# Two partial sums out of one PSUM bank: twelve value products and every sixth gate of a fused Fourier-mixing and gated feed-forward kernel

## The chip, the cores and the metric

The kernel runs on one core of one Trainium2 chip. The metric is device time of one launch in microseconds (µs), smaller is better. Engines are named as the profile names them: PE is the matrix engine and PEld its weight loads, DVE the vector engine, ACT the scalar engine, POOL is GpSimd, SP only issues DMAs. PSUM is the memory that PE writes its products into; the kernel splits it into eight banks of 128 × 512 float32.

## The reference

```
X   = real(fft(fft(x, axis=1), axis=2))      # x: 8 batches x 3008 rows x 256 channels
x2  = X.reshape(24064, 256)
out = (relu(x2 @ w_gate) * (x2 @ w_val)) @ w_out   # w_gate, w_val: 256 x 1536, w_out: 1536 x 256
```

## The kernel before, in words

**What one tile is.** The transform is kept as a cosine part U and a sine part V (128 channels by 1505 columns for each batch). A pair of mirrored output rows needs U+V and U−V, so the feed-forward weights are folded once at the start: WA acts on U, WB on V, and WM holds minus twice WB. The 1505 columns of a batch are cut in three blocks of 512, 512 and 481 columns, and the 1536 hidden features in NF = 12 groups `fi` of 128. One tile is one `fi` of one block: it makes gate and value for U+V and for U−V, takes relu(gate) times value, and writes 128 × (2·columns) bfloat16 of hidden values `h`. The finished block is multiplied by `wo` during the next block, eight output products (L781) for each tile.

**Batch 0** is done by `first_tile` and `single_tile` in four segments. There `gate` and `value` each make WA·U + WB·V in a bank (`two`, L874 and L875), the first half is read, and `mirror` (L880) adds the difference to the same bank for the second half.

**Batches 1 to 7** run in `slot(cur, mid, nxt, after, …)`, one call for each tile, 252 in all. `cur` is the tile whose value is made in this slot, `mid` the next one, `nxt` the one after it, whose gate is made now, and `after` the third. The engines take their instructions in exactly the order in which the Python code emits them (`manual_schedule`), so the call order inside `slot` is the order on each engine. On PE one slot is: `sine_part(nxt)` (WM·V into the only bank `g`, L1015), five output products, `cosine_part(nxt)` (WA·U added into a bank `p`, L1022), `mirror` of the tile before `cur` (L880), the two products of `value(cur)` into a bank `v`, three output products. There are two banks `p` and two banks `v`, used in turn.

The other engines follow. ACT copies `g` to memory as q (L1018), and `seed(after)` (L1010) writes the share of channel 128 (row `CB` times the weights `b2`) into the bank `p` that `after` will use; it has to wait until the bank's last tile was read. DVE first does `second` of the tile before `cur` (relu times value for U−V, read out of the bank `v` that `mirror` completed, L910), then `relu_mult(cur)` (the same for U+V, L910), then `both(nxt)` (L1026), which makes p − q/2. POOL adds q to that (L1027) and otherwise folds the rows of later batches. After the slots 0, 2, 6, 8, 12, 14, 18 and 20 of a batch three products (L585) of the next batch's transform follow, and DVE puts their results together later (L597). `keep_rest` (L905) copies the last 33 + 33 columns of a 481-column tile to the buffer LB by DMA.

One tile, (batch 1, block 0, `fi` 6), has the "kind" `"o"`: its gate is made as in batch 0, with three products. `gate_128` (L836, L837) makes `b2` once by twelve products of one column, read from row 0 of WB. `finish` handles the value half that is left over after the last slot.

Of the kernel before, what the change touches and what calls it, by code (L numbers as in the profile page):

```python
# [29 lines left out]
def dram(ap, offset, pattern):  # L30
    return bass.AP(ap.tensor, offset, [list(p) for p in pattern])
# [3 lines left out]
def kernel(  # L35
# [8 lines left out]
    nc = tc.nc  # L44
    B, S, D = x.shape
    DF = moe_w_gate.shape[1]
    NF = DF // 128
# [3 lines left out]
    NK = NE + NJ  # L51
# [230 lines left out]
    us = single("us", [128, 6])  # L282
    ums = single("ums", [128, 1])
    m2 = single("m2", [128, 1])
    half_pi = single("half_pi", [128, 1])
    kvec = single("kvec", [128, NK])
    dvec = single("dvec", [128, 129], pool=st_)
    go = single("go", [128, 2])
    c128p = single("c128p", [128, 2, 3, 2])
# [167 lines left out]
    for t in range(3):  # L457
        n = ROWS[1][t]
# [46 lines left out]
    b2 = single("b2", [128, NF])  # L505
    one = single("one", [1, 1], BF16)
    nc.vector.memset(one[:], 1.0)


    def even_table(n, c):  # L510
# [322 lines left out]
    def gate_128():  # L833
        p = psD.tile([128, 512], F32, name="d", tag="d")
        for f in range(NF):
            nc.tensor.matmul(p[:, f:f + 1], lhsT=WB[0][0:1, f * 128:(f + 1) * 128], rhs=one[:], start=True, stop=True)  # L836
        nc.vector.tensor_scalar(b2[:], p[:, 0:NF], scalar1=1.0, op0=ALU.mult, scalar2=None)  # L837
# [39 lines left out]
    def mirror(bank, st, i):  # L877

        W, v = (WB, st["vm"]) if st["b"] == 0 else (WM, st["vs"])
        nc.tensor.matmul(bank[:, 0:st["n"]], lhsT=W[i][:, st["f"]], rhs=v, start=False, stop=True, skip_group_check=True)  # L880

    def bank(tag):
        return {"g": psG, "p": psP, "v": psV, "d": psD}[tag].tile([128, 512], F32, name=tag, tag=tag)

    def space():
        return rp.tile([128, 512], F32, name="r", tag="r", bufs=12)

    def relu(st):
        st["r"] = space()
        nc.scalar.activation(st["r"][:, 0:st["n"]], st["g"][:, 0:st["n"]], ACTF.Relu)  # L890

    def half_h(st, sign):

        n = st["n"]
        return st["h"][:, 2 * n - 1:n - 1:-1] if sign else st["h"][:, 0:n]

    def mult(st, sign, r=None):
        n = st["n"]
        nc.vector.tensor_tensor(half_h(st, sign), (r or st["r"])[:, 0:n], st["v"][:, 0:n], op=ALU.mult)  # L899

    def keep_rest(st):
        o, h0 = 2 * REST * (st["b"] - 1) % 256, 896
        while h0 < 962:
            k = min(962 - h0, 256 - o)
            nc.sync.dma_start(out=LB[:, st["fi"], o:o + k], in_=st["h"][:, h0:h0 + k])  # L905
            o, h0 = 0, h0 + k

    def relu_mult(st, sign):
        n = st["n"]
        nc.vector.scalar_tensor_tensor(half_h(st, sign), in0=st["s"][1 + sign][:, 0:n], scalar=0.0, in1=st["v"][:, 0:n],  # L910
                                       op0=ALU.max, op1=ALU.mult)
# [28 lines left out]
    def single_tile(st, outs, extra=(), last=(), tag="p"):  # L940

        gate(st, tag)
        if pending is not None:
            finish(pending)
        value(st)
        mult(st, 0)
        run(todo_out, outs)
        for step in extra:
            step()
        mirror(st["g"], st, 0)  # L950
        relu(st)
        run(todo_out, outs)
        for step in last:
            step()
        return st

    def first_tile(st, extra, outs):
# [46 lines left out]

    def seed(st, p=None):

        if st is None or st["kind"] == "o":
            return
        st["p"] = p or bank("p")
        nc.scalar.activation(st["p"][:, 0:st["n"]], st["c"], ACTF.Copy, scale=b2[:, st["fi"]:st["fi"] + 1])  # L1010

    def sine_part(st):
        n = st["n"]
        st["g"] = bank("g")
        nc.tensor.matmul(st["g"][:, 0:n], lhsT=WM[0][:, st["f"]], rhs=st["vs"], start=True, stop=True)  # L1015
        q = space()
        st["s"] = q, space(), q
        nc.scalar.copy(q[:, 0:n], st["g"][:, 0:n])  # L1018

    def cosine_part(st):  # L1020
        n = st["n"]
        nc.tensor.matmul(st["p"][:, 0:n], lhsT=WA[0][:, st["f"]], rhs=st["us"], start=False, stop=True, skip_group_check=True)  # L1022

    def both(st):
        n, (q, sp, sm) = st["n"], st["s"]
        nc.vector.scalar_tensor_tensor(sp[:, 0:n], in0=q[:, 0:n], scalar=-0.5, in1=st["p"][:, 0:n], op0=ALU.mult, op1=ALU.add)  # L1026
        nc.gpsimd.tensor_tensor(sm[:, 0:n], sp[:, 0:n], q[:, 0:n], op=ALU.add)  # L1027

    def slot(cur, mid, nxt, after, outs, fold_us):

        stop = len(todo_out)

        def out(part):
            run(todo_out, len(todo_out) - stop + outs * part // 8)
        old = nxt is not None and nxt["kind"] == "o"
        new = nxt is not None and not old
        if old:
            gate(nxt)
        lead = cur["lead"]
        if lead:  # L1040
            out(5)
        if new and mid["kind"] != "o":
            sine_part(nxt)
        out(3 if not lead else 5)
        out(5)
        if new and mid["kind"] == "o":
            sine_part(nxt)
        if new:
            cosine_part(nxt)
        seed(after)  # L1050
        if pending is not None:
            mirror(pending["v"], pending, 1)
        if pending is not None:
            second(pending)
        value(cur)
        if cur["kind"] == "o":
            mult(cur, 0, cur["first"])
        else:
            relu_mult(cur, 0)
        if new:  # L1060
            both(nxt)
        if old:
            nxt["first"] = nxt["r"]
            mirror(nxt["g"], nxt, 0)
            relu(nxt)
        run_fold(fold_us)
        run_one(evict)
        run_one(sums)
        out(8)
        return cur  # L1070
# [142 lines left out]
```

## Time and profile before

| | |
|---|---|
| median of 3 runs | 631.26 µs (630.81 to 631.33) |
| the profiled execution: its own time | 630.98 µs |
| the profiled execution: its span, first to last instruction | 629.2 µs |
| busy: PE, DVE, POOL, ACT | 620.5, 551.5, 502.7, 445.5 µs |
| clock granted to PE, as a share of full speed | 1.000 |

The profile is of one execution. A timeline row gives the start in µs from the span's start, the busy time (of several merged instructions with "x3"), the engine, the line of the kernel, the operation, what it writes and reads, the sizes, and in brackets how long the engine had been idle and what ended that. The matmuls are pipelined: a 512-column product is shown 0.38 µs long, but the next one starts 0.22 µs after it, so it is the distance between starts that tells how full PE is. The last reader of a bank and the next writer are tied by a semaphore; a wait shows as a distance between starts that is longer than the products in it.

### The profile page before, as it was taken

Reading aid. Unit: us, or ns where it says so; the run is one execution under the profiler, and the core shown is the slowest. Engines: PE = TensorE matmul, PEld = TensorE weight load, DVE = VectorE, ACT = ScalarE, POOL = GpSimd, SP = SyncE. Lnnn points to the kernel's source line nnn. Section 1 sums busy time; section 2 is a strip of 40 time slices with the busy share of each in tenths; the row PEclk is TensorE's granted clock in tenths of the full one; section 3 lists DMA queues with packets and bytes.
Section 4 is the critical chain, followed back from the end, with each engine's and each line's share of the span. In section 5 each row is a group of like instructions: output and inputs, shape, how many; then the busy total and the mean of one; then the engine's idle time right before and its main releaser. Section 6 shows DMA issues by size and latency. Waiting matters only on the chain.

```text
span 629.2 us, 12441 instructions
## 1 busy us (share of the span) xinstructions
PE 620.5 (99%) x4114; PEld 398.4 (63%) x4114; DVE 551.5 (88%) x981; ACT 445.5 (71%) x813; POOL 502.7 (80%) x478
## 2 busy tenths in 40 slices
PE   8999999999999999999999999999999999999997
PEld 2566666566666666666666666666666666666666
DVE  8886676999899899988999999899999989999991
ACT  7796667777777767777777777777777777777762
POOL 8887992898999988799979989699886566666660
PEclk9999999999999999999999999999999999999999
DMA  9953748734264327315362426211221111211113
GB/s 240 209 206 118 173 177 102 182 73 151 82 150 145 126 76 183 113 44 165 83 187 64 140 76 130 68 50 36 77 61 38 42 60 56 57 38 51 51 44 102
DMA packets 82911, 66.47 MB, mean 106 GB/s; under 512 B 38517, under 2 KB 65941, under 8 KB 82846
## 3 DMA queue, kind: packets, MB, share of 16 engines
q1 hardware_dynamic: 78260, 60.01, 34.3%
q0 software_dynamic: 3984, 4.92, 3.9%
q10 hardware_dynamic: 602, 0.75, 0.4%
q8 instruction: 32, 0.52, 0.4%
q14 instruction: 33, 0.27, 0.2%
HBM read 41.88 MB, written 34.16 MB: 121 GB/s over the span
## 4 chain that ended last, share of the span: by engine, by line
PE 91%; DVE 4%; issue 2%; POOL 1%; DMA 1%; ACT 1%; DVEq 0%; ACTq 0%; POOLq 0%
PE o L781 36%; PE v L880 10%; PE v L875 9%; PE v L874 9%; PE g L1015 8%; PE p L1022 8%; PE d L585 4%; DVE h L910 2%; PE p L880 1%; PE p L874 1%; PE p L875 1%; DMA XG<-in_x_dram,gidx 1%; DVE h L899 1%; DVE r L1026 1%; POOL XG L120 1%
## 5 line engine op out<-in xcount | busy, mean ns | idle before, releaser
L1027 POOL TENSOR_TENSOR r<-r 128x512 f32<-128x512 f32 (+1 forms) x251 | 313.2, 1254 | 100.5 <-DVE r L1026 98.1
L910 DVE SCALAR_TENSOR_TENSOR h<-r,v 128x512 bf16<-128x512 f32 (+1 forms) x502 | 317.1, 673 | 39.2 <-PE v L880 26.5
L781 PE MATMUL o<-wo,h 128*128 128x256 bf16 x2172 | 330.6, 272 | 0.0
L781 PEld LDWEIGHTS <-h 128*128 128x128 bf16 x2220 | 216.7, 98 | 112.0 <-issue 1.3
L1010 ACT ACTIVATE p<-CB,b 128x512 f32<-128x512 bf16 (+1 forms) x251 | 171.8, 684 | 73.4 <-DVE r L1026 72.1
L1018 ACT COPY r<-g 128x512 f32<-128x512 f32 (+1 forms) x251 | 145.1, 578 | 66.5 <-PE g L1015 57.4
L1026 DVE SCALAR_TENSOR_TENSOR r<-r,p 128x512 f32<-128x512 f32 (+1 forms) x251 | 167.9, 669 | 0.9 <-ACT r L1018 0.9
L875 PE MATMUL v<-V,WB 128*128 128x512 bf16 (+3 forms) x296 | 108.6, 367 | 0.0
L874 PE MATMUL v<-U,WA 128*128 128x512 bf16 (+3 forms) x296 | 108.6, 367 | 0.0
L880 PE MATMUL v<-V,WM 128*128 128x512 bf16 (+1 forms) x252 | 94.4, 375 | 0.8 <-DVE h L910 0.4
L1015 PE MATMUL g<-V,WM 128*128 128x512 bf16 (+1 forms) x251 | 94.1, 375 | 0.5 <-ACT r L1018 0.4
L1022 PE MATMUL p<-U,WA 128*128 128x512 bf16 (+1 forms) x251 | 94.1, 375 | 0.2 <-ACT p L1010 0.2
L899 DVE TENSOR_TENSOR h<-r,v 128x376 bf16<-128x376 f32 (+2 forms) x90 | 46.2, 546 | 17.6 <-PE v L880 10.1
L874 PEld LDWEIGHTS <-WA 128*128 128x128 bf16 x348 | 33.9, 97 | 39.5 <-issue 10.4
L875 PEld LDWEIGHTS <-WB 128*128 128x128 bf16 x348 | 34.0, 98 | 34.3 <-DVE WB L431 0.6
L794 ACT COPY os<-o 128x512 f32<-128x512 f32 x92 | 52.6, 571 | 3.5 <-issue 3.0
L198 POOL TENSOR_TENSOR XG<-XG,XD 128x510 f32<-128x510 f32 x42 | 53.0, 1270 | 0.8 <-DMA XG<-xr 0.8
L890 ACT ACTIVATE r<-p 128x376 f32<-128x376 f32 (+1 forms) x80 | 38.0, 486 | 17.8 <-PE p L880 9.0
L206 POOL TENSOR_TENSOR AA<-XG 128x510 f32<-128x510 f32 x42 | 45.5, 1093 | 0.0
L1015 PEld LDWEIGHTS <-WM 128*128 128x128 bf16 x251 | 24.6, 98 | 5.7 <-issue 0.3
L1022 PEld LDWEIGHTS <-WA 128*128 128x128 bf16 x251 | 24.5, 98 | 3.7 <-issue 0.8
L880 PEld LDWEIGHTS <-WM 128*128 128x128 bf16 x253 | 24.8, 98 | 3.1
(186 smaller groups left out, 412.3 us busy)
## 6 DMA issues: line engine op xcount, KB each, us to landing
out_dram<-os SPq DMA_DIRECT2D x124, 128.0 KB
xr<-in_x_dram SPq DMA_DIRECT2D x12, 768.0 KB
XG<-xr SPq DMA_DIRECT2D x12, 768.0 KB
XD<-in_x_dram SPq DMA_DIRECT2D x15, 512.0 KB
out_dram<-os SPq DMA_DIRECT2D x35, 112.0 KB
XD<-in_x_dram SPq DMA_DIRECT2D x8, 448.0 KB
CB<-ch SPq DMA_DIRECT2D x7, 376.2 KB
out_dram<-os SPq DMA_DIRECT2D x13, 96.0 KB
```

The source lines that it names most:

```text
L198: e.tensor_tensor(XG[p, r, t, ::-1, 1:D], XG[p, r, t, ::-1, 1:D], XD[p, r, t, :, D - 1:0:-1], op=ALU.add)
L781: nc.tensor.matmul(st["p"][0:m, q, :], lhsT=lhs(f), rhs=wo[:, f, :], start=(f == 0 and not (early and q)), stop=(f == NF - 1), skip_group_ ...
L874: nc.tensor.matmul(bank[:, 0:st["n"]], lhsT=WA[i][:, st["f"]], rhs=st["us"], start=True, stop=False)
L875: nc.tensor.matmul(bank[:, 0:st["n"]], lhsT=WB[i][:, st["f"]], rhs=st["vs"], start=False, stop=True)
L880: nc.tensor.matmul(bank[:, 0:st["n"]], lhsT=W[i][:, st["f"]], rhs=v, start=False, stop=True, skip_group_check=True)
L910: nc.vector.scalar_tensor_tensor(half_h(st, sign), in0=st["s"][1 + sign][:, 0:n], scalar=0.0, in1=st["v"][:, 0:n], op0=ALU.max, op1=ALU.mult)
L1010: nc.scalar.activation(st["p"][:, 0:st["n"]], st["c"], ACTF.Copy, scale=b2[:, st["fi"]:st["fi"] + 1])
L1015: nc.tensor.matmul(st["g"][:, 0:n], lhsT=WM[0][:, st["f"]], rhs=st["vs"], start=True, stop=True)
L1018: nc.scalar.copy(q[:, 0:n], st["g"][:, 0:n])
L1022: nc.tensor.matmul(st["p"][:, 0:n], lhsT=WA[0][:, st["f"]], rhs=st["us"], start=False, stop=True, skip_group_check=True)
L1026: nc.vector.scalar_tensor_tensor(sp[:, 0:n], in0=q[:, 0:n], scalar=-0.5, in1=st["p"][:, 0:n], op0=ALU.mult, op1=ALU.add)
L1027: nc.gpsimd.tensor_tensor(sm[:, 0:n], sp[:, 0:n], q[:, 0:n], op=ALU.add)
```

## The change

Three things are made in another way, and a few steps are moved.

- **Twelve values.** In batches 6 and 7 the tiles with `fi` 5 and 11 ("short") make their value with two products instead of three. `seed_value` (ACT) writes the channel-128 share into the bank `v` at the end of the slot before; `value_cosine` adds WA·U at the very beginning of the tile's own slot and ACT copies twice that sum out as `a`; `value_sine` adds WV·V, where WV is a copy of WB with row 0 zero, made once by DVE from WM times −1/2 and kept in the buffer `kvec`. The bank then holds U+V's value, and `value_second` makes the other as `a` minus the bank (DVE) and multiplies it with the gate on POOL, which has put the relu there before. Neither `mirror` nor `second` is run for such a tile in the next slot (`rest_of_pending` leaves them out); `value_of_cur` runs the steps of `cur` itself.
- **One gate of six.** For `fi` 2 and 8 (except in block 0 of batch 1, where it is `fi` 5 and 9) the gate is made in the bank `p` alone ("copied"): `cosine_part` comes first in the slot, ACT copies twice the bank out, `add_sine` adds WB·V after the value's products, ACT copies the bank out again, and POOL subtracts. There are as many products as before; `both` and the bank `g` are not used.
- **b2** comes by three DMAs (rows 0 of WB to DRAM and back to all partitions) and an ACT copy; `gate_128` goes, and tile (1, 0, 6) is made like the others. Row 0 of WB is set to zero by POOL in batch 1.
- `weights(2)` starts one tile earlier, and in `single_tile` the results that wait for copying out are copied after the steps in `last`, not before them.

```diff
-    kvec = single("kvec", [128, NK])
+    kvec = single("kvec", [128, DF // 2])
...
+    b2 = single("b2", [128, 2 * NF])
+    brow = single("brow", [128, 2 * NF], BF16)
+    WV = kvec[:].bitcast(BF16)
...
-    more = {(0, i): [s] for i, s in enumerate(weights(1) + weights(2))}
+    more = {(0, i): [s] for i, s in enumerate(weights(1))}
+    for i, step in enumerate(weights(2)):
+        more.setdefault((0, 3 + i), []).append(step)
...
-    more[(2, 2)] = [gate_128]
-    more_1 = {}
+    more[(1, 1)].append(keep_128)
+    more[(1, 4)].append(get_128)
+    more[(2, 2)] = [lambda: nc.scalar.copy(b2[:], brow[:])]
+    for k in range(3):
+        f = slice(512 * k, 512 * k + 512)
+        more[(3, 2 * k + 1)] = [lambda f=f: nc.vector.tensor_scalar(WV[:, f], WM[1][:, f], scalar1=-0.5, op0=ALU.mult, scalar2=None)]
+    more_1 = {1: [lambda: nc.gpsimd.memset(WB[0][0:1, :], 0.0)]}
...
-                    st["kind"] = "o" if (b, blk, fi) == (1, 0, 6) else "n"
+                    st["copied"] = fi in (2, 8) and (b, blk) != (1, 0) or (b, blk, fi) in ((1, 0, 5), (1, 0, 9))
+                    st["short"] = b > 5 and fi in (5, 11)
...
+    def copy_cosine(st):
+        n, sp, sm = st["n"], space(), space()
+        st["s"] = sm, sp, sm
+        nc.scalar.mul(sm[:, 0:n], st["p"][:, 0:n], 2.0)
+    def add_sine(st):
+        n, (_, sp, sm) = st["n"], st["s"]
+        nc.tensor.matmul(st["p"][:, 0:n], lhsT=WB[0][:, st["f"]], rhs=st["vs"], start=False, stop=True, skip_group_check=True)
+        nc.scalar.copy(sp[:, 0:n], st["p"][:, 0:n])
+        nc.gpsimd.tensor_tensor(sm[:, 0:n], sm[:, 0:n], sp[:, 0:n], op=ALU.subtract)
+    def seed_value(st):
+        st["v"] = bank("v")
+        nc.scalar.activation(st["v"][:, 0:st["n"]], st["c"], ACTF.Copy, scale=b2[:, NF + st["fi"]:NF + st["fi"] + 1])
+    def value_cosine(st):
+        n, st["a"] = st["n"], space()
+        nc.tensor.matmul(st["v"][:, 0:n], lhsT=WA[1][:, st["f"]], rhs=st["us"], start=False, stop=True, skip_group_check=True)
+        nc.scalar.mul(st["a"][:, 0:n], st["v"][:, 0:n], 2.0)
+    def value_sine(st):
+        n = st["n"]
+        nc.tensor.matmul(st["v"][:, 0:n], lhsT=WV[:, st["f"]], rhs=st["vs"], start=False, stop=True, skip_group_check=True)
+    def value_second(st):
+        n = st["n"]
+        a = st["a"][:, 0:n]
+        nc.vector.tensor_tensor(a, a, st["v"][:, 0:n], op=ALU.subtract)
+        nc.gpsimd.tensor_tensor(half_h(st, 1), st["s"][2][:, 0:n], a, op=ALU.mult)
+        if n == 481:
+            keep_rest(st)
...
     def slot(cur, mid, nxt, after, outs, fold_us):
+        if cur["short"]:
+            value_cosine(cur)
+        if cur["lead"]:
...
+        else:
+            if copied:
+                cosine_part(nxt)
+                copy_cosine(nxt)
+            elif nxt is not None:
+                sine_part(nxt)
+            out(5)
+            if nxt is not None and not copied:
+                cosine_part(nxt)
+            seed(after)
+            rest_of_pending()
+            value_of_cur()      
+            if copied:
+                add_sine(nxt)
+            elif nxt is not None:
+                both(nxt)
+        if nxt is not None and nxt["short"]:
+            sm = nxt["s"][2][:, 0:nxt["n"]]
+            nc.gpsimd.tensor_scalar(sm, sm, scalar1=0.0, op0=ALU.max, scalar2=None)
+        if mid is not None and mid["short"]:
+            seed_value(mid)
```

The call `finish(pending)` after the last slot is as it was: it runs `mirror` and `second` for the very last tile, which is a short one now.

More of the change, by code (lines that the diff above doesn't have):

```diff
@@ L504 @@
     ch128 = nc.dram_tensor("ch128", (B, 4 * NJ + 1), BF16, kind="Internal").ap()
-    b2 = single("b2", [128, NF])
-    one = single("one", [1, 1], BF16)
-    nc.vector.memset(one[:], 1.0)
+    wrow = nc.dram_tensor("wrow", (2, DF), BF16, kind="Internal").ap()
+    b2 = single("b2", [128, 2 * NF])
+    brow = single("brow", [128, 2 * NF], BF16)
+    WV = kvec[:].bitcast(BF16)
     def even_table(n, c):
@@ L831, with keep_128, get_128 @@
         more.setdefault((1, 8 + seg), []).append(lambda seg=seg: minus_v(nc.scalar, seg))
[L833 to L837, printed above, removed]
-    more[(2, 2)] = [gate_128]
-    more_1 = {}
+    def keep_128():
+        for i in range(2):
+            nc.sync.dma_start(out=wrow[i:i + 1], in_=WB[i][0:1, :])
+    def get_128():
+        nc.sync.dma_start(out=brow[:], in_=dram(wrow, 0, [[1, 128], [128, 2 * NF]]), allow_slow_non_contiguous=True)
+    more[(1, 1)].append(keep_128)
[5 more added lines that the diff above has]
+    more_1 = {1: [lambda: nc.gpsimd.memset(WB[0][0:1, :], 0.0)]}
     for at, step in zip((-5, -4, -3, -2, -1, 7, 7, 8, 14, 17), channel_loads() + channel_turn()):
@@ L951, in single_tile @@
         relu(st)
-        run(todo_out, outs)
+        for _ in range(outs):
+            run_one(todo_out)
         for step in last:
             step()
+        run(todo_out, 0)
         return st
@@ L1005, in seed @@
     def seed(st, p=None):
[L1007 to L1010, printed above, removed]
+        if st is not None:
+            st["p"] = p or bank("p")
+            nc.scalar.activation(st["p"][:, 0:st["n"]], st["c"], ACTF.Copy, scale=b2[:, st["fi"]:st["fi"] + 1])
     def sine_part(st):
@@ L1034, in out @@
             run(todo_out, len(todo_out) - stop + outs * part // 8)
[L1035 to L1040, printed above, removed]
-            out(5)
[L1042 to L1048, printed above, removed]
-            cosine_part(nxt)
@@ L1050, in slot, with rest_of_pending @@
[L1050 to L1057, printed above, removed]
-        else:
[L1059 to L1065, printed above, removed]
+        def rest_of_pending():
+            if pending is not None and not pending.get("short"):
+                mirror(pending["v"], pending, 1)
+                second(pending)
@@ new lines, in value_of_cur @@
+        def value_of_cur():
+            if cur["short"]:
+                value_sine(cur)
+            else:
+                value(cur)
+            relu_mult(cur, 0)
+            if cur["short"]:
+                value_second(cur)
+        copied = nxt is not None and nxt["copied"]
+        if cur["short"]:
+            value_cosine(cur)
+        if cur["lead"]:
+            out(4)
+            sine_part(nxt)
+            rest_of_pending()
+            value_of_cur()
+            out(5)
+            cosine_part(nxt)
+            seed(after)
+            both(nxt)
+        else:
+            if copied:
+                cosine_part(nxt)
+                copy_cosine(nxt)
+            elif nxt is not None:
+                sine_part(nxt)
+            out(5)
+            if nxt is not None and not copied:
+                cosine_part(nxt)
+            seed(after)
+            rest_of_pending()
+            value_of_cur()
+            if copied:
+                add_sine(nxt)
+            elif nxt is not None:
+                both(nxt)
```

## The prediction

> **What bounds the kernel now.** I read the page's totals first, then the timeline of batch 7, where only the tile loop is left, engine by engine.
>
> ```profile
> PE 620.5 (99%) x4114; PEld 398.4 (63%) x4114; DVE 551.5 (88%) x981; ACT 445.5 (71%) x813; POOL 502.7 (80%) x478
> ...
> PEclk9999999999999999999999999999999999999999
> ```
>
> PE is busy for 99% at a full clock. How little slack the others leave is seen in one slot of batch 7, PE's rows first, then ACT, DVE and POOL:
>
> ```profile
> 560.23 0.38 PE L880 MATMUL v<-V,WM 128*128 128x512 bf16 x1
> ...
> 561.21 0.38 PE L1015 MATMUL g<-V,WM 128*128 128x512 bf16 x1
> 561.42 0.71 PE L781 MATMUL o<-wo,h 128*128 128x256 bf16 x5
> 561.97 0.38 PE L1022 MATMUL p<-U,WA 128*128 128x512 bf16 x1
> 562.18 0.38 PE L880 MATMUL v<-V,WM 128*128 128x512 bf16 x1
> ```
>
> ```profile
> 560.68 0.69 ACT L1010 ACTIVATE p<-CB,b 128x512 f32<-128x512 bf16 x1 [0.26 <-DVE r L1026]
> 560.72 1.28 DVE L910 SCALAR_TENSOR_TENSOR h<-r,v 128x512 bf16<-128x512 f32 x2
> 560.73 1.28 POOL L1027 TENSOR_TENSOR r<-r 128x512 f32<-128x512 f32 x1 [0.68 <-DVE r L1026]
> ...
> 561.68 0.59 ACT L1018 COPY r<-g 128x512 f32<-128x512 f32 x1 [0.30 <-PE g L1015]
> 561.92 0.68 DVE L1026 SCALAR_TENSOR_TENSOR r<-r,p 128x512 f32<-128x512 f32 x1
> ```
>
> One slot is 562.18 − 560.23 = 1.95 µs: five 512-column products at 0.21 to 0.22 and eight output products at 0.11. PE has no gap in it, so work taken from PE is gained in full and each new wait of PE is lost in full. I call the start of `mirror` (L880) zero of the slot: the next slot begins 0.98 later (561.21), `second` and `relu_mult` on DVE begin at 0.49, 0.64 each, and `both` ends at 561.92 + 0.68, 0.42 after the next `mirror`. Only then can ACT seed a bank `p`. How fast one engine wakes another, and how closely ACT packs its work, is seen where ACT is late, at the entry of batch 1:
>
> ```profile
> 105.00 0.62 ACT L1018 COPY r<-g 128x512 f32<-128x512 f32 x1
> ...
> 105.47 0.73 ACT L1010 ACTIVATE p<-CB,b 128x512 f32<-128x512 bf16 x1
> ...
> 105.66 0.38 PE L1015 MATMUL g<-V,WM 128*128 128x512 bf16 x1 [0.44 <-ACT r L1018]
> ...
> 106.10 0.62 ACT L1018 COPY r<-g 128x512 f32<-128x512 f32 x1
> ```
>
> The copy ends at 105.62 and PE starts at 105.66: about 0.05. ACT starts its next step 0.47 after a copy and 0.63 after a seed, although each lasts longer.
>
> **The short tiles: saved.** Twelve tiles make two value products for three. For the last one, though, `finish` still runs `mirror`, so eleven products go: 11 × 0.22 = 2.4 µs.
>
> **The short tiles: a wait on PE.** `seed_value(c)` takes the bank `v` of tile c−2, whose last reader is `second(c−2)`, and that runs in slot c−1, after its `mirror`. Counted from that `mirror`: `second` ends at 0.49 + 0.64 = 1.13; ACT 0.03 later seeds for 0.69 (the row at 560.68); PE wakes at 1.13 + 0.03 + 0.69 + 0.05 = 1.90. But `value_cosine(c)` is the first product of slot c, due at 0.98. PE waits 0.92, and everything queued behind it on PE (`sine_part`, five output products) waits too. The 0.98 of work between is all that covers the chain.
>
> **The knock-on.** In slot c DVE now has four steps in a row: `second`, `relu_mult`, the new subtraction, `both(c+2)`. From its `mirror`, `both` ends at 0.49 + 3 × 0.64 + 0.68 = 3.09, the seed behind it at 3.09 + 0.03 + 0.69, PE wakes at 3.86. The product that needs this seed is due after seven 512-column and sixteen output products, 3.26. So another 0.60 (part of it earlier, where the copied gate two tiles on starts its slot with a product that waits for the seed before). Then ACT has, behind that seed, the second copy of the copied gate, an output copy and q before PE may write `g` again: 0.63 + 0.47 + 0.47 + 0.59 + 0.05 = 2.21 after the seed's start, against 1.93 of PE's work: 0.28. Together 0.92 + 0.60 + 0.28 − 0.22 = +1.6 for a pair of a short and the following copied tile. Bounds: 0.7 if the first wait alone stays, 2.3 if ACT gets no air before the next pair. The eleven pairs: four in batch 7 and one in batch 6 as worked out, 8.2; three with 481 columns, where each step is a few per cent shorter, 4.4; three in batch 6 where a transform's three products give 0.48 more cover and DVE was already late, 3.4; less 0.2 for a wait of before that is swallowed. Sum +15.8, the saving included.
>
> **The copied gates.** Their `cosine_part` moves from 0.76 into the slot (561.97) to its start (561.21). The rows say when the seed is ready against that place, at the first and the last of the 28 slots of batches 1 to 5 concerned; the other two copied tiles of batch 1 stand behind transform products, which hide it:
>
> ```profile
> 129.09 0.69 ACT L1010 ACTIVATE p<-CB,b 128x512 f32<-128x512 bf16 x1 [0.60 <-DVE r L1026]
> ...
> 129.49 0.38 PE L1015 MATMUL g<-V,WM 128*128 128x512 bf16 x1
> ...
> 130.25 0.38 PE L1022 MATMUL p<-U,WA 128*128 128x512 bf16 x1
> ...
> 130.57 0.38 PE L880 MATMUL v<-V,WM 128*128 128x512 bf16 x1
> ...
> 450.54 0.37 PE L1022 MATMUL p<-U,WA 128*128 128x481 bf16 x1
> ...
> 450.84 0.38 PE L880 MATMUL v<-V,WM 128*128 128x512 bf16 x1
> ...
> 460.71 0.67 ACT L1010 ACTIVATE p<-CB,b 128x481 f32<-128x481 bf16 x1 [0.34 <-DVE r L1026]
> ...
> 461.24 0.37 PE L1015 MATMUL g<-V,WM 128*128 128x481 bf16 x1
> ```
>
> The seeds end 0.29 and 0.14 after the slot's start. All 28 read so sum to 6.5; with 0.05 of waking each, 7.9. What is given back: `mirror` now often waits for DVE in the same slot (130.57 is 0.32 after 130.25 and 450.84 is 0.30 after 450.54, where 0.21 would do); those 19 gaps hold 1.9 and vanish inside the new wait. Taking `both` off DVE in that slot moves no seed, since the seed hangs on the `both` of two tiles before. One more copied tile, the first of batch 6, adds 0.2. Net +6.2; bounds −1.9 (the seeds come in time, the gaps go) and +8.5 (nothing given back).
>
> **The last tile.** Its own first wait, at 481 columns and with five output products as cover, is 0.7, and a product is drawn forward (0.2). Then:
>
> ```profile
> 614.70 0.37 PE L880 MATMUL v<-V,WM 128*128 128x481 bf16 x1
> ...
> 615.17 1.23 DVE L910 SCALAR_TENSOR_TENSOR h<-r,v 128x481 bf16<-128x481 f32 x2 [1.02 <-PE v L880]
> ...
> 616.45 0.36 PE L880 MATMUL v<-V,WM 128*128 128x481 bf16 x1 [0.21 <-DVE h L910]
> 616.65 1.27 PE L781 MATMUL o<-wo,h 128*128 128x256 bf16 x10
> ```
>
> ```profile
> L905 SPq DMA_DIRECT2D LB<-h x96: 464/482/5022, 159.1 to 618.0; - x96
> ```
>
> ```profile
> h<-in_moe_w_gate_dram POOLq DMA_DIRECT2D x3, 256.0 KB, 5.6
> ```
>
> From 614.70: DVE's subtraction ends at 0.47 + 1.23 + 0.65 = 2.35. POOL multiplies into the second half of `h` (about 1.2, the row at 560.73 for 512 columns), 3.6. `keep_rest` then copies from `h`, and `finish` writes that half of `h` again, so its `second` waits for POOL and for the DMA's landing. That landing has no row: at least the 0.48 of issuing, at most the 5.6 of a load sixteen times as large; I take 2.0, near the low end because of the size. `second` ends at 3.6 + 2.0 + 0.65 = 6.3, and the tenth output product, which needs it, starts near 6.4 instead of 616.65 + 9 × 0.11 − 614.70 = 2.9. So +3.4, and +4.3 with the first wait; bounds 2.8 and 8.0. The Trainium skill ("DMA: Bandwidth & Descriptors", the section on the anatomy of one DMA) gives a fixed 2.0 µs for setup and completion; by it the term would be the same 3.4.
>
> **The rest.** `gate_128` goes:
>
> ```profile
> 64.29 0.45 PE L836 MATMUL d<-one,WB 1*128 1x1 bf16 x12
> ```
>
> −0.5, and tile (1, 0, 6) loses one product, −0.2. Copying results later at the entry of batch 1 lets the copy of 105.00 start earlier; of the 0.44 seen there and a like wait behind it, and of a wait for weights in batch 0, I take −1.1 (bounds 0 and −1.6). The three DMAs for `b2` are issued some ten tiles before ACT copies it, and the rest of SP's queue waits for its folds anyway; WV's three steps fall where DVE is not the last. Both at nothing; if `b2` landed late, ACT and PE would stand for up to the 5.6 of the load above.
>
> **Sum:** 15.8 + 6.2 + 4.3 − 0.5 − 0.2 − 1.1 = +24.5 on the profiled execution's 630.98, which lies 0.3 under the median: 655.5 µs (span about 653.7).
>
> **Rivals.** (a) *Faster:* the seeds land in time and no new wait arises. It needs `seed_value` to end by 0.98 after `mirror`, and the chain above gives 1.85 before waking; only if ACT or DVE were half as long does it turn. Then −2.4 − 0.5 − 0.2 − 1.1 − 1.9 − 0.2 = −6.3: 624.7. Chance 0.03. (b) *The copied gates cost nothing*, DVE's relief bringing the seeds forward: −1.9 instead of +6.2, 647.4. For it: DVE is 88% busy. Against: the seed's releaser in the rows is the `both` two tiles before. Chance 0.12. (c) *Only the first wait of each pair lasts*, the knock-on being taken up: 11 × 0.7 − 0.2 = 7.5 for 15.8, 647.2. Chance 0.12. (d) *ACT does not recover between pairs*, 2.3 each: +8, 663. ACT's 71% speaks against. Chance 0.09. (e) *The clock falls in the tail:* PE stands for some 2.5 before the tenth output product, and the 72 products after it at half clock would take 72 × 0.11 = 7.9 longer, 663.4. The trace shows a full clock through gaps of 0.44 and nothing longer after the start. The Trainium skill ("TensorE: Matmul & The Clock Gate", the section on why this matters for your kernels) wants no gap over about 3 µs; by it the case arises only if the landing takes over half a microsecond more than my 2.0. Chance 0.02. (f) *Some waits vanish, nothing measurable remains*: 0.01.
>
> **Numbers.** The forecast has 0.61: 655.5. The range 644 to 664 takes in (b), (c), (d) and (e) and leaves out (a), (f) and pairs of (b) and (c) together. A difference of 0.2%, about 1.3 µs, is what a measurement of this kernel can tell from none: faster 0.03, same 0.01, slower 0.96.
>
> **What would show it.** In the trace after: the first WA product into `v` of a short tile idle for 0.9 with ACT's `v` seed as releaser; the next copied tile's first product idle behind ACT's `p` seed; in batches 1 to 5 gaps of 0.2 to 0.35 at the start of slots 0 and 6 and the `mirror` gaps gone; near the end one output product waiting 2 µs or more for DVE. PE products 24 fewer. If PE shows no idle time before those products, the forecast is wrong; if it does but the time is near 647, (b) or (c) is right, told apart by which of the two gaps is missing.

## The result, and the profile after

The changed kernel takes 664.59 µs (median of four, 663.66 to 665.13) beside 631.25 (630.81 to 631.33): ratio 1.0528, 95% interval 1.051 to 1.0546. It is slower, as forecast, but by 33.3 µs instead of 24.5, and lies outside the range. The profiled execution took 665.13.

Page of the changed kernel, busy time and the granted clock in forty slices:

```profile
PE 628.6 (95%) x4045; PEld 399.2 (60%) x4090; DVE 533.4 (80%) x942; ACT 475.4 (72%) x880; POOL 536.2 (81%) x504
PEclk9999989999999999999999999999999999999997
```

PE is idle for 5% where it was idle for 1%, and the clock is no longer full in two places: in the sixth slice (83 to 100 µs) and at the end. The weight loads, 4,090 for 4,114, show the 24 products that went (some matmul records of this trace are missing, so the 4,045 can't be compared).

To see where the time went I split the run at two steps that every variant has. Mark 1 is the first `relu_mult` of batch 1; mark 2 is the pair `second`, `relu_mult` at the change from batch 5 to batch 6, in the slot of tile (6, 0, 0). Timeline, DVE's rows, of the kernel before:

```profile
107.29 0.68 DVE L910 SCALAR_TENSOR_TENSOR h<-r,v 128x512 bf16<-128x512 f32 x1
...
473.97 1.25 DVE L910 SCALAR_TENSOR_TENSOR h<-r,v 128x481 bf16<-128x481 f32 x2
```

and of the changed kernel:

```profile
112.52 0.68 DVE L919 SCALAR_TENSOR_TENSOR h<-r,v 128x512 bf16<-128x512 f32 x1
...
486.00 1.25 DVE L919 SCALAR_TENSOR_TENSOR h<-r,v 128x481 bf16<-128x481 f32 x2
```

Of the 34.15 between the two profiled executions (630.98 and 665.13), 5.2 arise before batch 1, 6.8 in batches 1 to 5, 22.1 in batches 6 and 7 with the tail.

**Before batch 1**, timeline of the changed kernel, rows of PE, DVE and POOL; L847 is the step that makes the minus half of the table (WV) in `kvec`, L206 a fold on POOL:

```profile
83.34 6.32 POOL L206 TENSOR_TENSOR AA<-XG 128x510 f32<-128x510 f32 x6
84.01 5.80 DVE L847 TENSOR_SCALAR kvec<-WM 128x512 bf16<-128x512 bf16 x1
...
89.62 0.42 POOL L251 TENSOR_TENSOR AA<-XG 128x6 f32<-128x6 f32 x2
...
91.69 0.47 PE L889 MATMUL v<-CB,WB 128*128 128x377 bf16 x1 [4.67 <-DVE h L908]
...
93.36 0.36 DVE L847 TENSOR_SCALAR kvec<-WM 128x512 bf16<-128x512 bf16 x1
...
98.91 0.28 DVE L847 TENSOR_SCALAR kvec<-WM 128x512 bf16<-128x512 bf16 x1
```

The same instruction on the same sizes took 5.80, 0.36 and 0.28. The long one ends 0.15 after POOL's six additions (83.34 + 6.32 = 89.66), while POOL has gone on at once with the two small ones of L251. The second starts in the last 0.2 of a fold on POOL (L222, from 91.91 to 93.57) and also ends 0.15 after it; the third runs where POOL does nothing. The DVE steps of the tiles queue behind it, and PE stands for 4.67. Windows of the same stretch (us, busy time of PE, PEld, DVE, ACT, POOL, granted clock, DMA):

```profile
84.00:88.00 4.00, 3.02 (x22) 1.91 (x20) 4.00 (x2) 2.15 (x5) 4.00 (x5) 1.00 0.28 98
88.00:92.00 4.00, 0.31 (x2) 0.15 (x2) 3.64 (x5) 0.00 (x0) 3.92 (x7) 0.96 0.57 139
92.00:96.00 4.00, 4.00 (x19) 2.32 (x18) 2.04 (x5) 1.36 (x3) 1.58 (x1) 0.61 1.06 341
```

After the gap the clock is 0.61 for one window of 4 µs.

**The waits that were forecast** are there. View of PE's waits in the changed kernel (in total, times, longest):

```profile
PE v L1058 <- ACT v L1054: 10.1, 12, 1.0
PE p L1033 <- ACT p L1021: 2.7, 16, 0.2
PE o L782 <- DVE h L919: 2.6, 1, 2.6
```

Twelve first waits of about 0.85 before `value_cosine` (L1058) behind the `v` seed (L1054); the copied gates' first product (L1033) behind the `p` seed (L1021); one wait of 2.6 near the end. A product is shown longer than the distance to the next one, so this view shows too little of short waits: by the distances between starts in the timeline, between mark 1 and mark 2, 29 gaps of 0.2 to 0.35 ahead of L1033 hold 8.2 in all. One first wait in the timeline, as the chain had it: `second` and `relu_mult` on DVE, the seed on ACT, PE:

```profile
574.79 1.28 DVE L919 SCALAR_TENSOR_TENSOR h<-r,v 128x512 bf16<-128x512 f32 x2
575.51 0.69 ACT L1054 ACTIVATE v<-CB,b 128x512 f32<-128x512 bf16 x1
576.25 0.38 PE L1058 MATMUL v<-U,WA 128*128 128x512 bf16 x1 [0.81 <-ACT v L1054]
```

**The tail**, timeline (POOL's product, the copy's issue, DVE's second step, PE), then windows:

```profile
645.34 1.21 POOL L1069 TENSOR_TENSOR h<-r 128x481 bf16<-128x481 f32 x1 [2.32 <-DVE r L1068]
646.58 0.47 SPq L914 DMA_DIRECT2D LB<-h  x1
648.44 0.66 DVE L919 SCALAR_TENSOR_TENSOR h<-r,v 128x481 bf16<-128x481 f32 x1 [3.28 <-DMA LB<-h]
649.16 0.40 PE L782 MATMUL o<-wo,h 128*128 128x256 bf16 x1 [2.59 <-DVE h L919]
649.34 5.33 PE L782 MATMUL v<-wo,h 128*128 128x256 bf16 x24
```

```profile
648.00:652.00 4.00, 2.84 (x14) 2.04 (x15) 0.66 (x1) 0.37 (x1) 0.00 (x0) 0.51 0.46 131
652.00:656.00 4.00, 4.00 (x26) 3.02 (x24) 0.00 (x0) 0.74 (x2) 0.00 (x0) 0.64 0.14 37
```

The copy's landing takes 648.44 − 646.58 = 1.86 from its issue (the prediction took 2.0). But behind the wait of 2.59 the clock is 0.51 and 0.64, and 24 output products take 5.33, where they take 2.78 in the kernel before.

### The profile page after: what moved, and what is told of

Its sections match the earlier page's. It is cut to its first block, busy times and chain, and to the rows that moved or that the text cites. A ratio compares the mean times of both kernels' runs of the same rounds, so it can differ in the third digit from the quotient of the medians.

```text
span 663.4 us, 12372 instructions
## 1 busy us (share of the span) xinstructions
PE 628.6 (95%) x4045; PEld 399.2 (60%) x4090; DVE 533.4 (80%) x942; ACT 475.4 (72%) x880; POOL 536.2 (81%) x504
## 3 DMA queue, kind: packets, MB, share of 16 engines
q1 hardware_dynamic: 81496, 60.04, 33.3%
## 4 chain that ended last, share of the span: by engine, by line
PE 62%; DVE 18%; ACT 8%; issue 7%; POOL 3%; DMA 1%; SPq 0%; DVEq 0%; POOLq 0%; ACTq 0%
PE o L782 23%; DVE h L919 10%; PE v L889 6%; PE p L1033 6%; DVE r L1037 6%; PE v L884 5%; PE g L1026 4%; PE v L883 4%; PE d L586 4%; ACT p L1021 3%; POOL r L1038 1%; PE p L1048 1%; ACT os L795 1%; PE p L889 1%; ACT r L1029 1%
## 5 line engine op out<-in xcount | busy, mean ns | idle before, releaser
L919 DVE SCALAR_TENSOR_TENSOR h<-r,v 128x512 bf16<-128x512 f32 (+1 forms) x493 | 311.8, 673 | 87.9 <-PE v L889 71.1
L1021 ACT ACTIVATE p<-CB,b 128x512 f32<-128x512 bf16 (+1 forms) x252 | 173.1, 687 | 58.2 <-DVE r L1037 55.2
L1029 ACT COPY r<-g 128x512 f32<-128x512 f32 (+1 forms) x210 | 121.5, 579 | 48.1 <-PE g L1026 41.9
L1037 DVE SCALAR_TENSOR_TENSOR r<-r,p 128x512 f32<-128x512 f32 (+1 forms) x210 | 140.5, 669 | 0.6 <-ACT r L1029 0.6
L884 PE MATMUL v<-V,WB 128*128 128x512 bf16 (+3 forms) x283 | 104.0, 367 | 2.1
L1033 PE MATMUL p<-U,WA 128*128 128x512 bf16 (+1 forms) x251 | 94.0, 374 | 4.9 <-ACT p L1021 2.7
L883 PE MATMUL v<-U,WA 128*128 128x512 bf16 (+3 forms) x245 | 89.5, 365 | 0.0
L1026 PE MATMUL g<-V,WM 128*128 128x512 bf16 (+1 forms) x209 | 78.3, 375 | 1.2
L908 DVE TENSOR_TENSOR h<-r,v 128x376 bf16<-128x376 f32 (+1 forms) x88 | 44.7, 542 | 17.4 <-PE v L889 9.3
L883 PEld LDWEIGHTS <-WA 128*128 128x128 bf16 x335 | 32.7, 98 | 37.2 <-issue 10.9
L206 POOL TENSOR_TENSOR AA<-XG 128x510 f32<-128x510 f32 x42 | 45.4, 1090 | 0.0
L1044 ACT ACTIVATE r<-p 128x512 f32<-128x512 f32 (+1 forms) x42 | 24.7, 589 | 22.1 <-PE p L1033 20.0
L1026 PEld LDWEIGHTS <-WM 128*128 128x128 bf16 x210 | 20.5, 98 | 16.4 <-issue 11.7
```

What stands on the lines that cost most here:

```text
L883: nc.tensor.matmul(bank[:, 0:st["n"]], lhsT=WA[i][:, st["f"]], rhs=st["us"], start=True, stop=False)
L884: nc.tensor.matmul(bank[:, 0:st["n"]], lhsT=WB[i][:, st["f"]], rhs=st["vs"], start=False, stop=True)
```

## The experiments

Each edit is made to the changed kernel (664.59) unless said otherwise; medians beside the kernel before, which ran between 630.66 and 631.49.

**1. WV by ACT.**

```diff
-        more[(3, 2 * k + 1)] = [lambda f=f: nc.vector.tensor_scalar(WV[:, f], WM[1][:, f], scalar1=-0.5, op0=ALU.mult, scalar2=None)]
+        more[(3, 2 * k + 1)] = [lambda f=f: nc.scalar.mul(WV[:, f], WM[1][:, f], -0.5)]
```

> The three steps that make the minus half of the value table (WV, 128x512 each) run on ACT instead of DVE, at the same three places; all else as in the changed kernel (664.6). Theory 1, the trace of the changed kernel: the first of these DVE steps took 5.80 us because DVE could not run it while GpSimd ran its six additions of 128x510 one behind the other; PE stood 4.7 and then ran at half clock for some microseconds, together about 6.2. On ACT the step has no such partner: about 0.6 each in ACT's idle time, no gap of PE over 1 us near 85-92, time about 658.4 (657.5 to 659.5). Theory 2: the step waited for its data or its target (the table WM still being written, kvec still being read): ACT would take as long at that place and the time would stay within 1 us of 664.6.

656.42 (655.42 to 657.35; ratio 1.0409, 1.0392 to 1.0427), 1.1 below the range given. The view of line L847 (duration in ns, first and last start):

```profile
L847 ACT ACTIVATE kvec<-WM x3: 631/632/632, 83.0 to 91.5; 128x512 bf16<-128x512 bf16 x3
```

At the same places and on the same data ACT needs 0.63 each time: theory 2 falls. The DVE steps at the two marks:

```profile
105.77 0.68 DVE L919 SCALAR_TENSOR_TENSOR h<-r,v 128x512 bf16<-128x512 f32 x1
...
479.26 1.25 DVE L919 SCALAR_TENSOR_TENSOR h<-r,v 128x481 bf16<-128x481 f32 x2
```

Batch 1 begins 112.52 − 105.77 = 6.75 earlier; that is the price of the step, with the low clock behind its gap. The other 3.0 of this execution (655.42 for 665.13) lie in the tail, below.

**2. WV on DVE, but later.**

```diff
-        more[(3, 2 * k + 1)] = [lambda f=f: nc.vector.tensor_scalar(WV[:, f], WM[1][:, f], scalar1=-0.5, op0=ALU.mult, scalar2=None)]
+        more[(3, 5 + k)] = [lambda f=f: nc.vector.tensor_scalar(WV[:, f], WM[1][:, f], scalar1=-0.5, op0=ALU.mult, scalar2=None)]
```

> The same three DVE steps, moved from tiles 1, 3 and 5 of the last segment of batch 0 to tiles 5, 6 and 7, where GpSimd has nothing to do in the trace of the changed kernel. Theory 1 (DVE shut out by GpSimd): each takes about 0.28, as the third one did, and the time is about 658.4, the same as with ACT. Theory 2 (data or target late): the first step waits at its new place less, but its duration, which starts after all its semaphores, stays several us. Theory 3 (any DVE step there delays the chain, however short): the time stays above 661, since three steps are still added to DVE.

658.03 (657.69 to 658.54; 1.0433, 1.0415 to 1.045). Timeline, POOL and DVE:

```profile
91.86 1.66 POOL L222 TENSOR_TENSOR G<-AA 128x762 bf16<-128x762 f32 x1
92.36 1.32 DVE L847 TENSOR_SCALAR kvec<-WM 128x512 bf16<-128x512 bf16 x1
...
95.43 0.28 DVE L847 TENSOR_SCALAR kvec<-WM 128x512 bf16<-128x512 bf16 x1
```

The time is the one theory 1 expected, and theory 3 falls; the profiled execution (657.69) is 2.3 above that of experiment 1, of which 1.2 is the clock in the tail (experiment 10). The first step did not take the 0.28 expected. My place was 1.2 too early: POOL was still in its last fold, until 93.52, and the first step ended 0.16 after it. That miss shows the mechanism once more, with another POOL instruction.

**3. Strided WV steps.**

```diff
-        f = slice(512 * k, 512 * k + 512)
-        more[(3, 2 * k + 1)] = [lambda f=f: nc.vector.tensor_scalar(WV[:, f], WM[1][:, f], scalar1=-0.5, op0=ALU.mult, scalar2=None)]
+        for j in range(2):
+            f = slice(512 * k + j, 512 * k + 512, 2)
+            more.setdefault((3, 2 * k + 1), []).append(lambda f=f: nc.vector.tensor_scalar(WV[:, f], WM[1][:, f], scalar1=-0.5, op0=ALU.mult, scalar2=None))
```

> The changed kernel with each of the three WV steps on DVE at its old place, but as two steps over every second column (256 elements, stride two) in place of one over 512 columns in a row. The third step of the changed kernel took 0.28 for 512 elements, more than an element per cycle of the rates seen elsewhere (0.64 to 0.69 for 512); a strided step should run at the lower rate, about 0.33 for 256. Theory A (only the fast form is shut out while GpSimd works): no step takes over 1 us, no long gap of PE near 86 us, 656.4 to 658.5. Theory B (any DVE step with both ends in SBUF is shut out): the first of them takes 5 us or more again, 664 to 665.

665.16 (664.78 to 665.66; 1.054, 1.0524 to 1.0556). Timeline:

```profile
83.04 6.33 POOL L206 TENSOR_TENSOR AA<-XG 128x510 f32<-128x510 f32 x6
83.69 6.06 DVE L848 TENSOR_SCALAR kvec<-WM 128x256 bf16<-128x256 bf16 x2
```

The time and the first step are those of theory B: half the elements at a lower rate (0.31 for 256 later on, where 512 took 0.28) are shut out just as long, the first of the two steps for 5.85. The tiles' own DVE steps, which read PSUM besides SBUF, ran beside the same six additions before the change, each 0.54 long:

```profile
83.66 6.32 POOL L206 TENSOR_TENSOR AA<-XG 128x510 f32<-128x510 f32 x6
85.91 1.00 DVE L899 TENSOR_TENSOR h<-r,v 128x377 bf16<-128x377 f32 x2
```

So what sets the shut-out step apart is not its stride. That both its ends lie in SBUF is the difference that these rows show; whether its operation (`tensor_scalar`) or its type counts as well was not tried.

**4. No short tiles.** `st["short"] = False`, and WV isn't made.

> No short tile at all, and the minus half of the value table is not made; copied gates and all the rest as in the changed kernel. The changed kernel's trace puts 14.9 on eleven short pairs (waits less the saved products), 7.0 on the last tile with its clock, 6.2 on the first WV step: 664.6 - 28.1 = 636.5 (635 to 638.5). By the prediction's own terms the short tiles cost 20.1 in all: 644.5; a time there would say that the WV step and the clock are not what was lost.

638.73 (638.37 to 639.39; 1.0126, 1.0109 to 1.0143), 0.2 above the range given. What I left out: the copied gates of batches 6 and 7 stay, and part of their wait I had booked on the pairs. Behind mark 2 this kernel takes 638.69 − 479.52 = 159.17, and 630.05 − 473.42 = 156.63 without copied gates (experiment 5): 2.5. The marks:

```profile
106.02 0.68 DVE L916 SCALAR_TENSOR_TENSOR h<-r,v 128x512 bf16<-128x512 f32 x1
...
479.52 1.25 DVE L916 SCALAR_TENSOR_TENSOR h<-r,v 128x481 bf16<-128x481 f32 x2
```

**5. Only the rest of the change.** Also `st["copied"] = False`.

> No short tiles, no minus half, no copied gates: of the change there remain the gate's bias row through memory in place of twelve small products, tile (1, 0, 6) in the new form, the later weights and the order of copies at the entry of batch 1. The prediction's terms: -0.5 -0.2 -1.1 = -1.8, so 629.2 beside 631.0 (bounds 630.3 and 628.7). The trace of the changed kernel showed less gain at the entry of batch 1 than that: by it about 630.2. If the time is 631.0 or above, the bias row's way through memory costs what it saves.

630.12 (629.86 to 630.7; 0.9986, 0.9977 to 0.9995): a small gain, 1.0, the smaller of the two expected.

```profile
106.00 0.68 DVE L916 SCALAR_TENSOR_TENSOR h<-r,v 128x512 bf16<-128x512 f32 x1
...
473.42 1.25 DVE L916 SCALAR_TENSOR_TENSOR h<-r,v 128x481 bf16<-128x481 f32 x2
```

Between the marks: 367.42 here, 373.50 with copied gates (experiment 4). Their price in batches 1 to 5, with the first one of batch 6, is 6.1. Some 0.4 of it is a wait for POOL's memset in batch 1 that the prediction did not have (shown under experiment 7).

**6. The copied gate's first product later.**

```diff
-            if copied:
-                cosine_part(nxt)
-                copy_cosine(nxt)
-            elif nxt is not None:
+            if nxt is not None and not copied:
                 sine_part(nxt)
             out(5)
+            if copied:
+                cosine_part(nxt)
+                copy_cosine(nxt)
+                out(8)
```

> In a copied gate's slot the product that waits for ACT's seed stands behind five output products instead of ahead of them, and the three last output products of the slot stand ahead of mirror, so that DVE has the same time as before; all else as in the changed kernel. Theory 1 (the seed arrives 0.14 to 0.29 us after the slot's start plus 0.05 of waking, and nothing else holds these slots): the 7.9 us of gaps in batches 1 to 5 go, in batches 6 and 7 the part of the knock-on that falls on this product (some 3), and up to 1.9 come back as gaps of mirror: 654 to 659, likeliest 656. Rival (DVE or ACT sets these slots, and the gap only moves to mirror or to the next product): above 661.

656.62 (655.84 to 657.0; 1.0399, 1.0384 to 1.0415): 8.0 less, where 8.6 likeliest was expected. The wait for the `p` seed is down from 2.7 in 16 places to

```profile
PE p L1033 <- ACT p L1021: 0.9, 5, 0.2
```

So nothing else held these slots; the rival falls.

**7. Copied gates alone, later.** Experiments 4 and 6 together, and WB's row zeroed one tile earlier (`more_1 = {0: ...}`), since POOL's memset was in the way at the entry of batch 1. Timeline of the changed kernel:

```profile
117.72 1.37 POOL L848 MEMSET WB<- 1x1536 bf16 x1
...
119.14 0.39 PE L1048 MATMUL p<-V,WB 128*128 128x512 bf16 x1 [0.45 <-POOL WB L848]
```

> No short tiles and no minus half; the copied gates with their first product behind five output products and the last three output products ahead of mirror; WB's row zeroed one tile earlier, ahead of POOL's additions. If the copied gate's whole cost was the place of its first product, its gaps go and mirror's small gaps of the kernel before go too: against 630.1 with the same rest and no copied gates, 1.0 to 1.4 less, 628.7 to 629.6. If the copied gate has a price of its own (its second copy on ACT, its subtraction on POOL), above 630.1.

627.88 (627.64 to 627.99; 0.9947, 0.9933 to 0.996): below the kernel before by half a per cent, and 0.8 below what I gave. The marks:

```profile
106.10 0.68 DVE L916 SCALAR_TENSOR_TENSOR h<-r,v 128x512 bf16<-128x512 f32 x1
...
471.81 1.25 DVE L916 SCALAR_TENSOR_TENSOR h<-r,v 128x481 bf16<-128x481 f32 x2
```

Batches 1 to 5 take 365.71: 1.7 less than without copied gates, 7.8 less than with the same gates in the old order. The first product's place, with some 0.45 from the memset, turns the copied gate from a loss into a gain. The gain is `mirror`'s small gaps given back: by the distances between starts, between the two marks, they hold 4.7 in experiment 5 and 2.8 here.

**8. The bank `d` for the short tiles of batch 7**, their seed one slot earlier.

```diff
-        st["v"] = bank("v")
+        st["v"] = bank("d" if st["b"] == 7 else "v")
...
-        if mid is not None and mid["short"]:
-            seed_value(mid)
+        for st, early in ((nxt, True), (mid, False)):
+            if st is not None and st["short"] and early == (st["b"] == 7):
+                seed_value(st)
```

> In batch 7 the short tile's value has the bank d, which nothing uses there, and its seed is issued a slot earlier; order of all else as in the changed kernel. By the prediction's chain (the first wait comes from the bank v, which second of two tiles before gives free too late) the first wait goes in the six tiles of batch 7: 0.95 x 5 + 0.73 = 5.5, of which the four DVE steps in a row may take some back later as knock-on, since no PE wait lies ahead of them any more: 659 to 662, likeliest 660. Rival (the wait is for ACT being busy, not for the bank): the waits stay, 664.6.

658.06 (653.77 to 658.76; 1.0411, 1.0378 to 1.0443), 6.5 less, 0.9 below the range given. The six waits of batch 7 are gone:

```profile
PE v L1058 <- ACT v L1054: 5.5, 6, 1.0
```

The first wait is the bank's, as the prediction's chain had it, and not ACT's being busy. The profiled execution (657.44) had a full clock in the tail, which is some 3 of its 7.7; why one other execution took only 653.77 stays open.

**9. The last tile long.** `... and (b, blk, fi) != (7, 2, 11)` at the end of `st["short"]`.

> The last tile (7, 2, 11) makes its value with three products as before the change; the other eleven short tiles stay. The prediction's term for this tile is 4.3 (first wait 0.7, a product drawn forward 0.2, the tail behind POOL's multiplication and the copy's landing 3.4); the trace of the changed kernel adds a half clock over some 24 output products behind the 2.8 us gap, about 2.7. If both hold, about 664.6 - 7.0 = 657.6, and the granted clock in the last 15 us is full. If the half clock has another cause than the gap, it stays and the time is about 660.3.

658.43 (657.6 to 659.03; 1.0436, 1.0419 to 1.0454): 6.2 less, and 6.9 less in the profiled execution (658.21), whose clock is 1.00 from 640 to 652. That is near the 657.6 expected, and not the 660.3 of another cause.

**10. No `finish` for the last short tile.** The call behind the loop is left out; the half that it writes again stays POOL's product.

> The last short tile's value is not made a second time behind the loop (finish is left out there; its second half is then POOL's product alone, as in the other eleven). The tenth output product then waits for POOL's product (about 3.6 us after mirror) and not for the copy's landing and DVE's second step (6.4): -2.8; and a gap under 1 us should leave the clock full, another -1.2 to -2.7: 659.2 to 660.6. If the clock falls in the tail without the 2.6 us gap, only the first part: 661.8. If the copy's landing is not what the tail waits for, no change.

660.11 (659.88 to 660.72; 1.0458, 1.0442 to 1.0474), 4.5 less. Timeline:

```profile
647.41 0.28 PE L782 MATMUL o<-wo,h 128*128 128x256 bf16 x1 [0.89 <-POOL h L1069]
647.53 2.78 PE L782 MATMUL v<-wo,h 128*128 128x256 bf16 x24
```

With a wait of 0.89 in place of 2.59 the 24 products take 2.78 in place of 5.33. A gap of 0.89 leaves the clock full. That a long gap alone does not decide is seen in experiments 1 and 2, whose tails are the same instructions. Experiment 1:

```profile
642.20 0.28 PE L782 MATMUL o<-wo,h 128*128 128x256 bf16 x1 [2.58 <-DVE h L919]
642.32 2.78 PE L782 MATMUL v<-wo,h 128*128 128x256 bf16 x24
```

Experiment 2:

```profile
643.19 0.39 PE L782 MATMUL o<-wo,h 128*128 128x256 bf16 x1 [2.59 <-DVE h L919]
643.38 3.99 PE L782 MATMUL v<-wo,h 128*128 128x256 bf16 x24
```

After the same gap: no loss, 1.2, and 2.6 in the changed kernel. In experiments 3 and 6 the 24 products take 4.27 and 4.21 after 2.55, in experiment 8 2.78 after 2.54. The four executions of experiment 1 fall into two pairs, 655.42 and 655.59 at a mean clock of 1.0, 657.26 and 657.35 at 0.997.

**11. Everything together.** Experiments 1, 6, 8 and 9, short tiles in batch 7 alone (five), the earlier memset, and DVE's subtraction behind `both`:

```diff
             relu_mult(cur, 0)
-            if cur["short"]:
-                value_second(cur)
...
                 both(nxt)
+        if cur["short"]:
+            value_second(cur)
```

> Everything that the traces asked for in one kernel: copied gates late as in the run before; short tiles in batch 7 alone and not the last tile, five of them, their value in bank d with the seed a slot earlier, DVE's subtraction behind both; WV by ACT; WB's row zeroed earlier. Theory: each first wait and each knock-on has its own remedy, so five products less are 1.1 us gained, of which the 0.15 before add_sine and the 0.3 before the next sine product may take back up to 2: 628 to 631, likeliest 629. Rival: the short tiles load ACT or DVE so much that some wait returns at each: 5 x 0.5 to 1.5 more, 632 or above.

628.23 (627.73 to 628.9; 0.9954, 0.9941 to 0.9968), within the range given, but no better than experiment 7, which has no short tile at all. In the slot behind a short tile PE has a gap again, ahead of `add_sine` (L1048):

```profile
555.82 0.38 PE L884 MATMUL v<-V,WB 128*128 128x512 bf16 x1
...
556.19 0.38 PE L1048 MATMUL p<-V,WB 128*128 128x512 bf16 x1
```

0.37 where 0.22 would do: the third value product that was saved is missing as cover for ACT's first copy. Five such gaps of 0.15 take 0.75 of the 1.1 gained, and four of 0.04 ahead of the next `sine_part` another 0.15.

**12. The three output products behind the value in those slots.**

```diff
                 copy_cosine(nxt)
-                out(8)
+                if not pending.get("short"):
+                    out(8)
...
             if copied:
+                out(8)
                 add_sine(nxt)
```

> As the kernel with everything (628.2), but where the tile before is a short one, so that its third value product no longer lies in the copied gate's slot, the three output products stay behind the value instead of ahead of it. If the 0.15 us gap that PE has ahead of add_sine in five such slots comes from ACT's copy being too close behind cosine_part, five gaps go: 0.75 less, 627.5, and the five short tiles are then gained (627.9 is the same kernel without them). Rival: the gap goes to the next product of the slot or to the next mirror, no change, 628.2.

628.06 (627.88 to 628.26; 0.9951, 0.9938 to 0.9965), no change. The rows say why:

```profile
555.15 0.38 PE L1033 MATMUL p<-U,WA 128*128 128x512 bf16 x1
...
555.80 0.49 PE L782 MATMUL o<-wo,h 128*128 128x256 bf16 x3
556.27 0.38 PE L1048 MATMUL p<-V,WB 128*128 128x512 bf16 x1
```

From `cosine_part` to `add_sine` 1.12 pass, as before the edit (1.13, from 555.06 to 556.19): the order within that stretch changed, not the work in it. My expectation had overlooked that; neither its theory nor its rival named it.

## Why the prediction was wrong, point by point

- **The step that failed: "WV's three steps fall where DVE is not the last. Both at nothing."** The first step cost 6.75 (experiment 1, mark 1). I had looked at DVE's queue and not at what POOL does in those tiles. The six additions in a row stand in the trace of before as well, from 83.66, and a DVE step from SBUF to SBUF has no row beside them; the prediction should have given this step two bounds, as it did for the other steps without a row. The Trainium skill ("SBUF — State Buffer", the section "Who interferes with whom") says that a `tensor_scalar` of DVE that uses its second pair of ports, which GpSimd shares, and a GpSimd instruction exclude each other: whoever starts first has the pair for its whole instruction. The trace agrees that DVE is shut out, and that DVE steps with an operand in PSUM are not. For how long when GpSimd's instructions follow each other the section does not say: here it was 5.80, through the rest of six instructions 1.05 apart, and not the rest of one.
- **Rival (e), the clock in the tail, with a chance of 0.02, came in.** I had tied it to a gap over about 3 µs; it came at 2.59, and three of the four executions show the mean clock of the profiled one, 0.992 (the fourth 0.995, 663.66). Profiled, it cost 3.0: 665.13 − 486.00 = 179.13 behind mark 2, against 655.42 − 479.26 = 176.16 in experiment 1, whose tail ran at full clock. The Trainium skill ("TensorE: Matmul & The Clock Gate", the section on why this matters for your kernels) wants no gap over about 3 µs; the traces differ from it, since gaps of 2.55 to 2.59 were not safe here. The loss was smaller than the 7.9 of the rival, since the clock was full again after some 5 µs.
- **The short tiles and the last tile: right.** Predicted +15.8 and +4.3: 20.1. Experiment 1 against experiment 5 behind mark 2: 176.16 − (630.05 − 473.42) = +19.5. Experiments 8 and 10 show the two chains, bank and landing, as they were worked out. The 15.8 holds a small slip: five pairs at 1.6 are 8.0, not 8.2. The 2.0 for the landing, 1.86 measured, was a choice between 0.48 and 5.6; the section of the Trainium skill that the prediction names for it speaks of DMAs that GpSimd issues, and this one is issued by SP.
- **The copied gates: right.** Predicted +6.2, measured 6.1 (experiments 4 and 5); (b) falls. The gaps ahead of the first product hold 8.2 (7.9 and 0.2 were predicted). `mirror`'s gaps give back more than the 1.9 predicted, 2.5 (4.7 in experiment 5, 2.2 in the changed kernel), and the memset's 0.45 makes up for that by luck. Experiment 6 shows that the place of the one product carries it.
- **The rest: half as large.** Predicted −1.8, measured −1.0 (experiment 5). Batch 1 begins 107.29 − 106.00 = 1.3 earlier there, but 0.55 is left of it at mark 2; what takes the difference in batches 1 to 5 stays open.
- **Sum** on the profiled executions: 6.75 for the step, 3.0 for the clock, 0.9 less gained by the rest, −0.7 on the other two, −0.2 by which experiment 1 reaches mark 1 before experiment 5: 9.7, the distance from the forecast's 655.5 to 665.13. Rivals (c) and (d) would have moved the term that came out right.

## What to carry to other kernels

Before a step is called free on an engine, look at the engine that can shut it out as well as at its own queue: here the same DVE instruction cost 0.28 beside an idle POOL and 5.80 beside a busy one, and on ACT 0.63 at each of three places. An accumulation that starts from a seeded bank puts the seed's whole chain ahead of its first product, so that product belongs behind work that needs no seed: the same gates cost 6.1 with it first, and earned 1.7 with it behind five output products (0.45 of the difference is the memset's). And in a pipeline where PE covers the other engines' latencies, a product saved is cover lost too; five products saved were worth nothing measurable.

## What the runs showed of the hardware that was not expected

- A DVE step with source and target in SBUF, 0.28 long alone, took 5.80 when it began during the first of six POOL additions in a row. It ended 0.15 after the sixth, while POOL had gone on at once with two additions of six columns. Begun 1.2 before the end of a fold it took 1.32; two strided steps of half the size took 6.06 beside the six additions. DVE steps that read PSUM as well did not wait: 0.54 each beside the same six.
- The granted clock fell after gaps of 4.67 (0.61 over the next 4 µs) and of 2.59 (0.51), and not after 0.89. Among six profiled executions with a gap of 2.54 to 2.59 ahead of the same 24 products, two kept a full clock (2.78) and four did not (3.99 to 5.33). What decides between these was not tried.
